# Layer two's weights placed first, the low part issued last, fewer idle products, last stores on three queues

## The chip, the cores and the metric

One core of one Trainium2 chip runs the kernel. Times are device microseconds of one execution; of several runs the median is shown. A profile of one execution was taken beside them.

## The reference

The input `x` has 4 sequences of 4096 tokens with 192 channels, 16384 tokens in all. Three stages follow one another:

```
w = softmax(weight)                                     # 8 heads x 7 taps
x = causal convolution of x with w, each head on its 24 channels
x = (sigmoid(x @ w_gate) * (x @ w_val)) @ w_out         # layer one: 192 -> 1536 -> 192
out = relu(x @ w_in2) ** 2 @ w_out2                     # layer two: 192 -> 2048 -> 192
```

All of it is float32.

## The kernel before

**Precision.** A float32 operand is split into a high part (rounded to the array's fp32r format) and a low part (the rest). A product is taken as high x high, high x low and low x high, which is why each weight tile holds high and low halves and each activation two tensors (`gh` and `gl` for the hidden values).

**Tiling.** 32 tiles of 512 tokens. Layer one goes through 12 *units* of 128 hidden channels for a tile, layer two through 8 units of 256. A unit has a *row* part (`rows`, L477: from the 192 channels to the hidden values, 9 steps) and a *column* part (`cols`, L531: from the hidden values back to 192 channels, 5 steps for each 128 hidden channels, so 5 in layer one and 10 in layer two). Each step is a pair of products, one for partitions 0 to 63 and one for 64 to 127, which run side by side on the array. The two halves sum in different PSUM banks (`acc`, A for output channels 0 to 127, B for the rest), and `fold` (L555) adds them at the end of a phase: ScalarE (ACT) copies one, VectorE (DVE) adds the other, for A and for B, and a third copy and add join B's halves.

**Order.** A phase is all units of one layer for one tile. Layer one runs five phases ahead; then phases of layer one (tile t) and layer two (tile t-5) alternate, and five phases of layer two end the kernel. The main loop (L753) takes unit e: its row products, then `activate`, then the column products that are due, then the *side work* of e. Columns run two units behind: at the first unit of a phase all pending columns of the phase before are run (and its `fold`), at the second none, after that one unit's per unit. PE, ACT and DVE each run their instructions in the order of issue.

`activate` (L518) takes per 128 hidden channels a sigmoid or relu on ACT, a multiplication on DVE (`times`), the high part on ACT (`high`, L508) and the low part on DVE (`low`, L514):

```
for s in acts:
    u.hidden.append(high(s))
    low(u.hidden[-1])
```

Side work is put on units by hand (`side`, `put`, L623 to L628):
- the convolution of the next input tile: a transpose, a first tap on ACT and six taps on DVE, for channels 0 to 127 (A) and, every second tile, for the last 64 channels of two tiles (B): 8 or 16 operations spread over the free units up to `part_at - 1`;
- its high part (ACT), low part (DVE) and `spread` (three DMAs on SyncE's queue, SP, that copy the parts to the other partitions: `x<-x`) at `part_at = at - 4` and the two units behind, where `at` is the first unit of its layer-one phase; loads of the input after it are issued at `part_at`;
- the same parts for layer two's input, on units 4 to 6 of the phase ahead;
- the conversion of layer two's weights (16 jobs of ACT and DVE steps), from unit 2 of the second tile to layer two's first phase. Layer one's weights are converted during the first 12 units, by `convert_and_activate`.

**Memory.** The pool `cp` lays its tiles out in the order of the first request. `w1` (L107) holds layer one's weights, 12 slices of 4608 bytes a partition. Layer two's eight places `u0` to `u7` (`weights2`, `place_of`, L113 to L119; 6144 bytes each) also hold raw weights and scratch while layer one's are converted, so the first request for `u0` to `u4` comes from those loads, behind the small tiles `cw`, `cwr`, `halos`, `xTA`, `xTB`, `gap` and `warm`; the nine small tiles of `conv_weights` (L283) come next, and then `u5` to `u7`.

**Start and end.** PE runs idle products on zeros (`run_idle`, three, then four behind the small products of `conv_weights`) before its first real work, the convolution of the first tiles by products with diagonal matrices (L396). At the end `evac2` (L578) folds, transposes A and B on DVE and stores them by six DMAs on SP.

Of the kernel before, what the change touches and what calls it, by code (L numbers as in the profile page):

```python
# [8 lines left out]
F32 = mybir.dt.float32  # L9
# [4 lines left out]
ALU = mybir.AluOpType  # L14
PSUM = bass.MemoryType.PSUM

P = 128
HB = 64
NT = 512
BLK = 32  # L20
HALVES = (slice(0, HB), slice(HB, P))
# [4 lines left out]
def kernel(  # L26
# [23 lines left out]
    nc = tc.nc  # L50
# [66 lines left out]

    def place_of(i, nm):
        return cp.tile([P, NW2], U32, tag=f"u{i}", name=nm)  # L119

    NRAW = NU2 - 3

# [160 lines left out]
    def conv_weights():  # L283


        mx, z, th, a, b, e, s, r, w = (
            cp.tile([H, k], F32, name=nm)
            for nm, k in (
                ("cmx", 1), ("cz", K), ("cth", K), ("ca", K), ("cb", K), ("ce", K),
                ("cs", 1), ("cr", 1), ("cn", K),  # L290
            )
        )
        nc.vector.tensor_reduce(out=mx, in_=cwr, op=ALU.max, axis=mybir.AxisListType.X)
        nc.vector.tensor_scalar(out=z, in0=cwr, scalar1=mx, scalar2=None, op0=ALU.subtract)
        nc.scalar.activation(th, z, AF.Tanh, scale=0.5)
        nc.vector.tensor_scalar(
            out=b, in0=th, scalar1=-1.0, scalar2=1.0, op0=ALU.mult, op1=ALU.add
        )
        nc.vector.tensor_scalar_add(a, th, 1.0)
        nc.vector.reciprocal(b, b)  # L300
        nc.vector.tensor_tensor(e, a, b, op=ALU.mult)
        nc.vector.tensor_reduce(out=s, in_=e, op=ALU.add, axis=mybir.AxisListType.X)
        nc.vector.tensor_scalar_add(s, s, 1e-9)
        nc.vector.reciprocal(r, s)
        nc.vector.tensor_scalar(out=w, in0=e, scalar1=r, scalar2=None, op0=ALU.mult)
        taken = banks.take("cwp")
        for i in range(2):
            nc.tensor.matmul(
                taken[1][:, i * K : (i + 1) * K], sel[:, i, :], w, start=True, stop=True
            )  # L310
        nc.scalar.copy(cw.rearrange("p i k -> p (i k)"), taken[1][:, 0 : 2 * K])
        banks.give(taken)
# [23 lines left out]
    def load_a(t, eng=None):  # L336
        xin[t] = xp.tile([P, NT], F32, tag="xiA", name="xiA")
        for cb in range(P // BLK):
            load_block(t, xin[t][cb * BLK : (cb + 1) * BLK], cb, eng)
# [168 lines left out]
    def high(s):  # L508
        v = Hidden()
        v.s, v.gh = s, gp.tile([P, NT], F32R, tag="gh", name="gh", bufs=5)  # L510
        nc.scalar.copy(v.gh, s)  # L511
        return v

    def low(v):  # L514
        v.gl = gp.tile([P, NT], F32R, tag="gl", name="gl", bufs=5)
        nc.vector.tensor_tensor(v.gl, v.s, v.gh.bitcast(F32), op=ALU.subtract)  # L516

    def activate(u):  # L518

        u.hidden, acts = [], []  # L520
        for i in range(1 if u.kind == 1 else 2):
            acts.append(act(u, i))
            times(u, acts[-1])
        banks.give(*u.banks)
        for s in acts:
            u.hidden.append(high(s))
            low(u.hidden[-1])

    acc = {}

    def cols(u):  # L531

        key = (u.kind, u.t)
        if u.f == 0:
            acc[key] = [[banks.take(f"acc{nm}") for nm in "AB"] for _ in HALVES]
        sums = acc[key]
        for i, v in enumerate(u.hidden):
            if u.kind == 1:  # L540
                w, lo = w1[:, u.f, NR:], N1 + HB
            else:
                w, lo = weights2(u.f)[1][:, i, :], NO + HB
            wa, wb, wl = w[:, 0:P], w[:, P : 2 * P], w[:, lo : lo + P]
            steps = ((0, wa, v.gh), (0, wa, v.gl), (0, wl, v.gh), (1, wb, v.gh), (1, wb, v.gl))
            first, last = u.f == 0 and i == 0, u.last and i == len(u.hidden) - 1
            for k, (b, wt, m) in enumerate(steps):
                for h, half in enumerate(HALVES):
                    nc.tensor.matmul(  # L549
                        sums[h][b][1], wt[half], m[half],  # L550
                        start=(first and k in (0, 3)), stop=(last and k in (2, 4)),
                    )
        return u.last

    def fold(key, dst_a, dst_b, own):  # L555

        (a0, b0), (a1, b1) = acc.pop(key)
        ca = op.tile([P, NT], F32, tag="c", name="ca")
        cb = op.tile([P, NT], F32, tag="c", name="cb")
        nc.scalar.copy(ca, a1[1])  # L560
        nc.scalar.copy(cb, b1[1])
        nc.vector.tensor_tensor(ca if dst_a is None else dst_a, a0[1], ca, op=ALU.add)
        nc.vector.tensor_tensor(cb, b0[1], cb, op=ALU.add)
        banks.give(a0, b0, a1, b1)
        tb = op.tile([P, NT], F32, tag="oB", name="tb")
        dst_b = cb if dst_b is None else dst_b
        nc.scalar.copy(tb[HALVES[own]], cb[HALVES[1 - own]])
        nc.vector.tensor_tensor(dst_b[HALVES[own]], cb[HALVES[own]], tb[HALVES[own]], op=ALU.add)
        return ca, cb

    def evac1(t):
# [6 lines left out]
    def evac2(t):  # L578

        t0 = tokens(t)  # L580
        ya, yo = fold((2, t), None, None, 0)

        def store(src, cb):
            nc.sync.dma_start(
                out=out[t0 : t0 + NT, cb * BLK : (cb + 1) * BLK].rearrange(
                    "(n t) c -> t n c", t=BLK
                ),
                in_=src.rearrange("t (n c) -> t n c", c=BLK),
            )

        def a():
            o = op.tile([P, NT], F32, tag="oA", name="oA")
            nc.vector.transpose(o, ya)
            for cb in range(P // BLK):
                store(o[cb * BLK : (cb + 1) * BLK], cb)

        def b():
            o = op.tile([P, NT], F32, tag="oB", name="oB")
            nc.vector.transpose(o[0:HB], yo[0:HB])
            for cb in range(HB // BLK):  # L600
                store(o[cb * BLK : (cb + 1) * BLK], P // BLK + cb)

        return [a, b]

# [31 lines left out]
    with tc.manual_schedule():  # L636
# [2 lines left out]
        warm = cp.tile([1, 1], F32, name="warm")  # L639
        nc.gpsimd.memset(warm, 0.0)  # L640
        nc.scalar.activation(warm, warm, AF.Sigmoid)
        load_a(0)
        nc.scalar.dma_start(out=unit, in_=eye)
        load_b(0, nc.gpsimd)
        conv = [convert1(f) for f in range(NU1)]
        for u in range(NU2):
            conv += [convert_rows2(u), convert_cols2(u)]

        idle = gp.tile([P, NT], F32, tag="s", name="idle")
        nc.gpsimd.memset(idle, 0.0)  # L650
        taken = banks.take("idle")

        def run_idle(n):
            for _ in range(n):
                nc.tensor.matmul(taken[1], idle[:, 0:P], idle, start=True, stop=True)  # L655

        for f in range(NRAW):
            conv[f].load()
        load_a(1, nc.gpsimd)
        run_idle(3)  # L660
        conv_weights()
        run_idle(4)
        banks.give(taken)
        a0, b0, (high0, low0, spread0) = prep_x(0, False, True)
        a1, _, parts1 = prep_x(1, True)
# [22 lines left out]
        a1[0]()  # L688
        diagonals(0)

        begin, end = where[1, 1, 2], where[2, 0, NU2 - 2] - 1
        for i, job in enumerate(conv[NU1:]):
            at = begin + i * (end - begin) // (2 * NU2 - 1)
            for s, ops in enumerate(job.stages):
# [6 lines left out]
        for t in range(2, NTILE):  # L701
            at = where[1, t, 0]
            before = starts[starts.index(at) - 1]
            a, b, parting = prep_x(t)
            taps = [o for ab in zip(a, b) for o in ab] if b else a
            part_at = at - 4
            put(taps, free, part_at - 1)
            for i, o in enumerate(parting):
                side[part_at + i].append(o)
            free = part_at + 2  # L710
            if t + 1 < NTILE:
                side[part_at].append(lambda t=t: load_a(t + 1))
                if t % 2:
                    side[part_at].append(lambda t=t: load_b((t + 1) // 2))
# [38 lines left out]
        for e, u in enumerate(units):  # L753
            rows(u)
            if e < NU1:
                convert_and_activate(e, u)
            else:
                activate(u)
            for o in stores:
                o()  # L760
            stores = []
            k = e - max(s for s in starts if s <= e)
            due = len(pending) if k == 0 else 0 if k == 1 else len(pending) - 1
            for _ in range(due):
                v = pending.popleft()
                if cols(v):
                    stores += (evac1 if v.kind == 1 else evac2)(v.t)
            pending.append(u)
            for o in side[e]:
                o()  # L770
        while pending:
            v = pending.popleft()
            if cols(v):
                for o in evac2(v.t):
                    o()
# [39 lines left out]
```

## Time and profile before

| | us |
|---|---|
| median of 3 runs (lowest, highest) | 2420.38 (2417.86, 2421.68) |
| profiled execution, its own time | 2419.86 |
| its span, first to last instruction | 2418.1 |
| PE busy | 2389.6 (99%) |
| PE weight loads (PEld) busy | 1930.4 (80%) |
| DVE busy | 1700.8 (70%) |
| ACT busy | 1301.3 (54%) |

Busy time is the union of an engine's records. A product's record lasts 0.39 us while the next pair starts 0.23 us behind it, so a busy PE says little on its pace; the distance from start to start does. The clock granted to PE (PEclk) is 1.00 at 2.4 GHz and 0.50 at 1.2 GHz.

### The profile page before, as it was taken

What the parts mean: (1) busy time and instruction counts of PE and PEld (TensorE: products, weight loads), DVE (VectorE), ACT (ScalarE), POOL (GpSimd) and SP (SyncE); (2) the same over time, 40 slices, a digit from 0 to 9 for tenths busy, and PEclk for the clock granted to TensorE, in tenths of its full rate; (3) what the DMA queues carried; (4) which work ended last, traced back from release to release, by engine and by line L of the source; (5) the groups of instructions that cost most, each with busy time, mean ns of one, the idle gap of its engine ahead of it and who ended that gap; (6) DMA issues with size and microseconds to landing.
All of it is one profiled execution on the core that took longest, in us unless ns stands there. A gap on an engine that the chain in (4) does not pass through costs nothing.

```text
span 2418.1 us, 49307 instructions
## 1 busy us (share of the span) xinstructions
PE 2389.6 (99%) x20526; PEld 1930.4 (80%) x20526; DVE 1700.8 (70%) x2676; ACT 1301.3 (54%) x2260; POOL 31.6 (1%) x98
## 2 busy tenths in 40 slices
PE   8999999999999999999999999999999999999998
PEld 5677788888888888888888888888888888888886
DVE  7777777777677676676767677776776766666776
ACT  6555555555455555555555555554555555555664
POOL 1000000000000000000000000000000000000000
PEclk9999999999999999999999999999999999999999
DMA  6222221121210111121111211112101111101111
GB/s 154 52 58 50 58 43 24 29 42 25 42 38 21 36 38 30 38 42 22 32 29 38 42 31 26 38 25 43 38 21 36 38 29 38 34 21 27 40 28 27
DMA packets 226896, 92.13 MB, mean 38 GB/s; under 512 B 202856, under 2 KB 214256, under 8 KB 226672
## 3 DMA queue, kind: packets, MB, share of 16 engines
q1 hardware_dynamic: 226272, 88.39, 17.2%
q8 instruction: 160, 2.62, 0.5%
q0 software_dynamic: 256, 0.52, 0.1%
q14 instruction: 64, 0.52, 0.1%
q10 hardware_dynamic: 144, 0.07, 0.0%
HBM read 26.03 MB, written 12.58 MB: 16 GB/s over the span
## 4 chain that ended last, share of the span: by engine, by line
PE 91%; DVE 4%; ACT 2%; issue 1%; DMA 0%; POOL 0%; SPq 0%; DVEq 0%; ACTq 0%; POOLq 0%
PE pg L489 27%; PE accA L549 24%; PE ph L489 22%; PE accB L549 17%; PE pv L489 2%; DVE s L506 1%; ACT gh L511 1%; DVE cvA L387 1%; PE cv L396 1%; DMA x<-x 0%; DVE cvB L387 0%; ACT s L502 0%; DVE gl L516 0%; PE idle L655 0%; ACT cvq L149 0%
## 5 line engine op out<-in xcount | busy, mean ns | idle before, releaser
L549 PE MATMUL accA<-gh,w 64*128 64x512 f32 x3584 | 955.5, 389 | 0.0
L489 PE MATMUL pg<-x,w 64*128 64x512 f32 x3456 | 854.1, 389 | 6.7 <-ACT w L178 3.2
L489 PE MATMUL pv<-x,w 64*128 64x512 f32 x3456 | 851.2, 389 | 7.9 <-DVE s L506 4.4
L511 ACT CAST gh<-s 128x512 fp32r<-128x512 f32 x896 | 555.8, 622 | 544.6 <-DVE s L506 537.9
L516 DVE TENSOR_TENSOR gl<-s,gh 128x512 fp32r<-128x512 f32 x896 | 608.2, 692 | 279.8 <-ACT gh L511 257.7
L489 PEld LDWEIGHTS pg<-x,w 64*128 64x128 f32 x3456 | 635.7, 185 | 130.3 <-ACT w L178 7.0
L549 PEld LDWEIGHTS accA<-gh,w 64*128 64x128 f32 x3584 | 647.5, 184 | 82.3 <-issue 4.5
L489 PEld LDWEIGHTS pv<-x,w 64*128 64x128 f32 x3456 | 635.8, 185 | 35.7 <-DVE s L506 12.7
L489 PE MATMUL ph<-x,w 64*128 64x512 f32 x4608 | 621.2, 391 | 0.0
L489 PEld LDWEIGHTS ph<-x,w 64*128 64x128 f32 x4608 | 471.1, 184 | 102.7
L549 PE MATMUL accA<-gl,w 64*128 64x512 f32 x1792 | 546.3, 389 | 0.4 <-DVE gl L516 0.2
L549 PE MATMUL accB<-gl,w 64*128 64x512 f32 x1792 | 545.9, 389 | 0.0
L549 PE MATMUL accB<-gh,w 64*128 64x512 f32 x1792 | 545.6, 388 | 0.0
L506 DVE TENSOR_TENSOR s<-s 128x512 f32<-128x512 f32 x512 | 330.2, 686 | 157.5 <-ACT s L502 155.9
L502 ACT ACTIVATE s<-ph 128x512 f32<-128x512 f32 x512 | 277.4, 594 | 216.3 <-PE ph L489 215.9
L506 DVE TENSOR_TENSOR s<-pv,s 128x512 f32<-128x512 f32 x384 | 263.2, 686 | 146.0 <-ACT s L502 145.4
L549 PEld LDWEIGHTS accB<-gh,w 64*128 64x128 f32 x1792 | 323.6, 184 | 37.4
L549 PEld LDWEIGHTS accA<-gl,w 64*128 64x128 f32 x1792 | 323.7, 184 | 37.2 <-DVE gl L516 1.1
L549 PEld LDWEIGHTS accB<-gl,w 64*128 64x128 f32 x1792 | 323.1, 184 | 37.5
L502 ACT ACTIVATE s<-pg 128x512 f32<-128x512 f32 x384 | 228.4, 595 | 204.1 <-PE pg L489 192.9
L387 DVE SCALAR_TENSOR_TENSOR cvA<-xTA,cw,cvA 128x512 f32<-128x512 f32 x186 | 138.7, 745 | 3.9 <-ACT cvA L383 3.7
L560 ACT COPY ca<-accA 128x512 f32<-128x512 f32 x64 | 37.3, 583 | 71.6 <-PE accA L549 71.6
(79 smaller groups left out, 758.2 us busy)
## 6 DMA issues: line engine op xcount, KB each, us to landing
x<-x SPq DMA_DIRECT2D x192, 256.0 KB, 3.8
out_dram<-oA SPq DMA_DIRECT2D x128, 64.0 KB, 1.9
xiA<-in_x_dram SPq DMA_DIRECT2D x124, 64.0 KB, 2.8
raw<-in_moe_w_out_dram SPq DMA_DIRECT2D x28, 192.0 KB, 3.5
out_dram<-oB SPq DMA_DIRECT2D x64, 64.0 KB, 1.9
xiB<-in_x_dram SPq DMA_DIRECT2D x60, 64.0 KB, 2.4
raw<-in_moe_w_in_dram SPq DMA_DIRECT2D x16, 192.0 KB, 4.1
raw<-in_moe_w_gate_dram SPq DMA_DIRECT2D x12, 192.0 KB, 3.4
```

Source lines behind the costliest of these rows:

```text
L387: nc.vector.scalar_tensor_tensor(out=st["cv"], in0=st["x"][:, k : k + NT], scalar=cw[:, i, k : k + 1], in1=st["cv"], op0=ALU.mult, op1=ALU ...
L396: nc.tensor.matmul(st["cv"], diagonal(i, k), st["x"][:, k : k + NT], start=(k == 0), stop=(k == K - 1),)
L489: nc.tensor.matmul(u.banks[h][1], w[half, o + c * P : o + (c + 1) * P], xs[1][half, place[n] + p, :], start=(i == 0), stop=(i == len(steps ...
L502: nc.scalar.activation(s, u.banks[i][1], AF.Sigmoid if u.kind == 1 else AF.Relu)
L506: nc.vector.tensor_tensor(s, u.banks[1][1] if u.kind == 1 else s, s, op=ALU.mult)
L511: nc.scalar.copy(v.gh, s)
L516: nc.vector.tensor_tensor(v.gl, v.s, v.gh.bitcast(F32), op=ALU.subtract)
L549: nc.tensor.matmul(sums[h][b][1], wt[half], m[half], start=(first and k in (0, 3)), stop=(last and k in (2, 4)),)
L560: nc.scalar.copy(ca, a1[1])
```

## The change

Five edits. The eight places are requested right behind the definition of `place_of`. `low` is no longer issued in `activate` but at the end of the unit's iteration, behind its due columns, folds and side work (from unit 12 on; the first 12 keep their order). Two idle products go, and the tile of zeros is written on DVE ahead of the first loads. The parts of a tile move from `at - 4` to `at - 5`, and the conversions of layer two begin at unit 8 of the second tile. For the very last unit the column steps are sorted so that B's come first, `fold` then takes B first, and the last six stores go to SP, ACT and POOL.

```diff
+    for u in range(NU2):
+        place_of(u, "free")
...
     def activate(u):
-        u.hidden, acts = [], []
+        acts = []
...
-        for s in acts:
-            u.hidden.append(high(s))
-            low(u.hidden[-1])
+        u.hidden = [high(s) for s in acts]
...
+        order = []
         for i, v in enumerate(u.hidden):
...
+            first = u.f == 0 and i == 0
+            order += [
+                (0, wa, v.gh, first), (0, wa, v.gl, False), (0, wl, v.gh, False),
+                (1, wb, v.gh, first), (1, wb, v.gl, False),
+            ]
+        if u is units[-1]:
+            order.sort(key=lambda step: -step[0])
...
-    def fold(key, dst_a, dst_b, own):
+    def fold(key, dst_a, dst_b, own, b_first=False):
...
+        def sum_a():
+            nc.scalar.copy(ca, a1[1])
+            nc.vector.tensor_tensor(dst_a, a0[1], ca, op=ALU.add)
+
+        def sum_b():
+            nc.scalar.copy(cb, b1[1])
+            nc.vector.tensor_tensor(cb, b0[1], cb, op=ALU.add)
+
+        def join():
+            nc.scalar.copy(tb[HALVES[own]], cb[HALVES[1 - own]])
+            nc.vector.tensor_tensor(
+                dst_b[HALVES[own]], cb[HALVES[own]], tb[HALVES[own]], op=ALU.add
+            )
+
+        for o in (sum_b, join, sum_a) if b_first else (sum_a, sum_b, join):
+            o()
...
-                store(o[cb * BLK : (cb + 1) * BLK], cb)
+                eng = nc.scalar if final and cb % 2 else nc.sync
+                store(o[cb * BLK : (cb + 1) * BLK], cb, eng)
...
-                store(o[cb * BLK : (cb + 1) * BLK], P // BLK + cb)
+                eng = nc.gpsimd if final and cb % 2 else nc.sync
+                store(o[cb * BLK : (cb + 1) * BLK], P // BLK + cb, eng)
...
+        idle = gp.tile([P, NT], F32, tag="s", name="idle")
+        nc.vector.memset(idle, 0.0)
         load_a(0)
...
-        idle = gp.tile([P, NT], F32, tag="s", name="idle")
-        nc.gpsimd.memset(idle, 0.0)
...
+        run_idle(2)
+        conv_weights()
         run_idle(3)
-        conv_weights()
-        run_idle(4)
...
-        begin, end = where[1, 1, 2], where[2, 0, NU2 - 2] - 1
+        begin, end = where[1, 1, 8], where[2, 0, NU2 - 2] - 1
...
-            part_at = at - 4
+            part_at = at - 5
...
             for o in side[e]:
                 o()
+            if e >= NU1:
+                for v in u.hidden:
+                    low(v)
```

## Rows read from the trace of the kernel before

**Rows 1.** The page, busy time: us, share of the span, number of instructions.
```profile
PE 2389.6 (99%) x20526; PEld 1930.4 (80%) x20526; DVE 1700.8 (70%) x2676; ACT 1301.3 (54%) x2260; POOL 31.6 (1%) x98
```
**Rows 2.** Windows: stretch, length, busy us of PE, PEld, DVE, ACT, POOL, clock, DMA.
```profile
74.70:322.48 247.78, 236.92 (x1967) 185.88 (x1964) 185.14 (x326) 132.04 (x237) 4.17 (x16) 0.99 0.22 51
322.48:2228.20 1905.72, 1905.72 (x16643) 1557.91 (x16641) 1329.15 (x2031) 1013.00 (x1754) 20.09 (x64) 1.00 0.16 33
2228.20:2408.56 180.36, 180.36 (x1560) 145.80 (x1558) 126.19 (x195) 105.38 (x184) 0.00 (x0) 1.00 0.14 30
...
118.00:162.00 44.00, 41.47 (x342) 33.07 (x341) 30.28 (x54) 23.06 (x41) 0.50 (x3) 0.96 0.27 58
```
**Rows 3.** Timeline of PE, phase starts: start us, us, engine, line, operation, tiles.
```profile
982.20 0.39 PE L489 MATMUL pg<-x,w 64*128 64x512 f32 x1
...
1022.56 0.63 PE L489 MATMUL ph<-x,w 64*128 64x512 f32 x3
...
1055.50 0.39 PE L489 MATMUL pg<-x,w 64*128 64x512 f32 x1
```
**Rows 4.** Timeline of PE: columns of units 3 and 5 start, rows of 6.
```profile
1044.41 0.62 PE L549 MATMUL accA<-gh,w 64*128 64x512 f32 x2
...
1046.74 0.62 PE L489 MATMUL ph<-x,w 64*128 64x512 f32 x3
...
1048.83 0.39 PE L549 MATMUL accA<-gh,w 64*128 64x512 f32 x1
...
1053.23 0.39 PE L549 MATMUL accA<-gh,w 64*128 64x512 f32 x1
```
**Rows 5.** Timeline of DVE, ACT and PE at the same layer-two phase's start.
```profile
1026.93 1.29 DVE L516 TENSOR_TENSOR gl<-s,gh 128x512 fp32r<-128x512 f32 x2
1028.14 0.69 DVE L562 TENSOR_TENSOR y<-accA,ca 128x512 f32<-128x512 f32 x1
...
1030.11 0.69 DVE L568 TENSOR_TENSOR yb<-cb,tb 64x512 f32<-64x512 f32 x1 [0.69 <-ACT tb L567]
1030.81 0.75 DVE L387 SCALAR_TENSOR_TENSOR cvB<-xTB,cw,cvB 128x512 f32<-128x512 f32 x1
...
1027.40 0.58 ACT L560 COPY ca<-accA 128x512 f32<-128x512 f32 x1
...
1031.36 0.62 PE L549 MATMUL accA<-gl,w 64*128 64x512 f32 x2
```
**Rows 6.** Timeline of DVE and PE at the layer-one phase's start behind it.
```profile
1064.64 0.68 DVE L568 TENSOR_TENSOR cb<-cb,tb 64x512 f32<-64x512 f32 x1 [0.69 <-ACT tb L567]
...
1066.38 0.39 PE L549 MATMUL accA<-gl,w 64*128 64x512 f32 x1
```
**Rows 7.** Waits of PE, 74.7 to 334 us: us in total, times, longest.
```profile
PE pv L489 <- DVE s L506: 4.4, 8, 0.8
PE pv L489 <- DMA x<-x: 3.0, 4, 0.9
PE pg L489 <- DMA x<-x: 2.6, 5, 1.1
```
**Rows 8.** Timeline of PE at the start; DMA engines' busy tenths, 0 to 30 us.
```profile
4.60 5.30 PE L655 MATMUL idle<-idle 128*128 128x512 f32 x6 [4.60 <-POOL idle L650]
...
13.91 6.17 PE L396 MATMUL cv<-xTB,diag 128*128 128x512 f32 x14
...
24.54 0.28 PEld L489 LDWEIGHTS pv<-x,w 64*128 64x128 f32 x1 [0.76 <-DMA x<-x]
...
DMA  0037999899999999999999999998509799888900
```
**Rows 9.** Timeline of DVE and SP's queue at the end; a POOL transfer's landing.
```profile
2411.96 0.69 DVE L593 STREAM_TRANSPOSE oA<-ca 128x512 f32<-128x512 f32 x1
...
2414.72 0.97 SPq L584 DMA_DIRECT2D out_dram<-oB  x2
...
xiB<-in_x_dram POOLq DMA_DIRECT2D x4, 64.0 KB, 2.7
```

More of the change, by code (lines that the diff above doesn't have):

```diff
@@ L544, in cols @@
             wa, wb, wl = w[:, 0:P], w[:, P : 2 * P], w[:, lo : lo + P]
[L545 to L552, printed above, removed]
+            first = u.f == 0 and i == 0
[5 more added lines that the diff above has]
+            order.sort(key=lambda step: -step[0])
+        ends = {step[0]: k for k, step in enumerate(order)} if u.last else {}
+        for k, (b, wt, m, first) in enumerate(order):
+            for h, half in enumerate(HALVES):
+                nc.tensor.matmul(
+                    sums[h][b][1], wt[half], m[half], start=first, stop=ends.get(b) == k,
+                )
         return u.last
-    def fold(key, dst_a, dst_b, own):
+    def fold(key, dst_a, dst_b, own, b_first=False):
         (a0, b0), (a1, b1) = acc.pop(key)
@@ L559, in fold @@
         cb = op.tile([P, NT], F32, tag="c", name="cb")
[L560 to L563, printed above, removed]
+        tb = op.tile([P, NT], F32, tag="oB", name="tb")
+        dst_a = ca if dst_a is None else dst_a
+        dst_b = cb if dst_b is None else dst_b
+        def sum_a():
[8 more added lines that the diff above has]
+                dst_b[HALVES[own]], cb[HALVES[own]], tb[HALVES[own]], op=ALU.add
+            )
+        for o in (sum_b, join, sum_a) if b_first else (sum_a, sum_b, join):
+            o()
         banks.give(a0, b0, a1, b1)
[L565 to L568, printed above, removed]
         return ca, cb
@@ L580, in evac2, with store @@
         t0 = tokens(t)
-        ya, yo = fold((2, t), None, None, 0)
-        def store(src, cb):
-            nc.sync.dma_start(
+        final = t == NTILE - 1
+        ya, yo = fold((2, t), None, None, 0, b_first=final)
+        def store(src, cb, eng):
+            eng.dma_start(
                 out=out[t0 : t0 + NT, cb * BLK : (cb + 1) * BLK].rearrange(
```

## The prediction

> **What bounds the kernel now.** I read the page's engine line first: PE is busy for 2389.6 of 2418.1 us, so what counts is the pitch of its products and the gaps between them [rows 1]. The windows come second. From 322.48 to 2228.20 us PE has no gap at all; from 74.70 to 322.48 it is busy for 236.92 of 247.78 us [rows 2]. Two losses hide beneath the 99%, and both show only when pairs are counted. A "pair" is one weight slice on both row halves.
>
> *Pitch.* The code issues 178 pairs from the first row product of a layer-one phase (982.20) to that of the next layer-two phase (1022.56): 40.36 us, 226.7 ns a pair. From there to 1055.50 it issues 142, in 32.94 us: 232.0 ns [rows 3]. The same array at the same clock is slower in layer two, and the step-by-step rows say where: the ten column pairs of unit 3 take 2.33 us (1044.41 to 1046.74), those of unit 5 take 2.27 (1053.23 to 1055.50) [rows 3, 4]. Only the weight tile differs. By the tile sizes (rounded up to 32 bytes) units 0 to 4 begin 60128 bytes behind the first byte of `w1`, plus multiples of 6144: 224 past a multiple of 512. The nine small tiles of `conv_weights` come in between, so units 5 to 7 begin on a multiple of 512, like every slice of `w1`. The slow ones are the ones off it.
>
> *Gaps.* 982 pairs belong to the stretch 74.70 to 322.48: at 226.7 ns 222.6 us, so 25.2 are lost, 0.75 of them to the pitch of its one layer-two phase. The waits there name DMA x<-x (3.0 and 2.6 us) and DVE s (4.4) [rows 7]. Idle understates it, since a record lasts 0.39 us and the pitch is 0.227; I share the 24.4 us out in proportion: 13.4 to the spread DMAs, 11.0 to the rest.
>
> **The change part by part.** The sum is made against the profiled execution, 2419.86 us (span 2418.1), 0.5 below the median of the three shown.
>
> *Weights ahead.* With the eight places requested right behind `w1` (55296 bytes, 108 x 512) and 6144 = 12 x 512 each, every slice of layer two starts on a multiple of 512 from `w1`. The small tiles have the same sizes and follow in the same order, so the pools behind them start where they did. A layer-two phase behind a layer-one phase then takes 142 x 0.2267 = 32.19 us instead of 32.94: 0.75 x 27 = 20.2. At the end only layer two runs: (1560 - 3) / 2 = 778 pairs (a window counts some three records that only reach into it) in 180.36 us, 176.4 at 226.7: 4.0 [rows 2]. Together **-24.2**. Units 5 to 7's row pairs are slow too, though aligned: unit 6's nine take 2.09 us (1046.74 to 1048.83) [rows 4]. They stand between the columns of units 3 and 4, whose late weight loads run on into them, so I count them as cured. Bounds: 0 if the address isn't the cause, -25 at most.
> The Trainium skill, "TensorE: Matmul & The Clock Gate", Part 2, gives the weight load a read port of its own that takes nothing from the running product, with a time that depends on the number of columns; by it this edit is worth 0 (first rival). The 2.33 against 2.27 us of rows 4 disagrees.
>
> *Low part last.* `activate` issued times, high, low; now low stands on DVE behind the unit's folds and side work. Inside a phase that is free or better: a unit's columns run two units later (over 6 us), and DVE fills its wait for the high part. At a phase start it isn't. In layer two's unit 0, before: gl at 1026.93, then the fold's y add at 1028.14 and yb at 1030.11, then a tap at 1030.81; PE wants the first gl at 1031.36 [rows 5]. After: the fold no longer waits for gl (ca ends at 27.40 + 0.58 = 27.98, so the fold is 0.15 earlier, and 0.05 more from the faster row products); its successor starts 0.70 behind yb, at 1030.61. With a tap in front (0.75, [rows 5]) the first gl ends at 1030.61 + 0.75 + 0.69 = 1032.05; PE, with 27 pairs 5.3 ns shorter, wants it at 1031.21: 0.84 late. Without a tap: 0.09. `put` spreads the 16 operations of an even tile over 18 units and one falls on this one; the 8 of an odd tile miss it. I add 0.1 for the restart (my estimate). Of the 26 such starts after the first, 12 have a tap, 14 none: 12 x 0.95 + 14 x 0.2 = **+14.2**. Behind gl times of unit 1 waits, 1.3 us later than now, but its columns come two units later. At a layer-one start behind layer two the fold's last add (1064.64 + 0.68) leaves 1066.38 - 1065.32 = 1.06 us for one gl of 0.69 and no DVE side work falls there [rows 6]: nothing. Bounds: 0 if folds end earlier than I think, +20 if every start loses what a tapped one does (26 x 0.95, less what the backlog gives back).
>
> *The stretch to 322 us.* `part_at` moves one unit forward, 247.78 / 68 = 3.6 us; the longest wait for the spread was 1.1 [rows 7], so the 13.4 goes. It moves the loads of the next input with it, ahead of the spreads on SP as before. Of the other 11.0 half goes: DVE has work during the high part, but where ACT holds the activation behind a conversion and a part, the order on ACT is as it was. Against it: gl late at six phase starts. With 1.06 us of room and 0.69 for gl, two transposes cost 1.0, one tap 0.4, two taps 1.1, one tap 0.4, three conversion steps (about 1.1 together, an estimate from their share of the tap's width) 0.7, and at the first layer-two start those and a tap 2.0, with restarts 6.2. Net -13.4 - 5.2 + 6.2 = **-12.4**. Bounds -24.4 and +6. Conversions, their raw loads on SP included, start six units later and end at the same unit; same work, so nothing, and if the denser order jams DVE, that is inside the bounds.
>
> *Start.* Idle products, 3 + 4, become 2 + 3, and their zeros are written on DVE, which otherwise waits for the first load, not behind POOL's four issues. Six passes took 5.30 us from 4.60 [rows 8]; four from about 1.4 end at 5, so the convolution on the array can begin up to 5 us before 13.91. But the first unit's row products ended on a DMA x<-x at 24.54, and the DMA engines are 9 tenths busy from 3 us to 20.25 (slices of 0.75 us) with raw weights, which an earlier spread only queues behind. What can go is their gap before the third spread: the slices reading 8, 5 and 0, 0.75 x (0.2 + 0.5 + 1.0) = **-1.3** [rows 8]. Nearest to a DMA bound, so I take that; bounds -5 (all of the array's lead counts) and +1 (the clock's later rise).
>
> *End.* The last unit's B columns come first and end six pairs, 1.36 us, before the last product. Their copy, add, copy, add (0.58 + 0.69 + 0.58 + 0.69, after the ACT and DVE rows of [rows 5]) end 1.2 us behind it, A's add 1.9; A's transpose starts there and not behind all five steps at 2411.96: 1.2 gained. Six issues on SP ran until 2415.69, 3 us past the transpose; on three queues they take half that, but a POOL transfer needs 2.7 us to land, where the kernel ended 2.4 behind SP's last issue [rows 9]. **-2.4**, bounds -3.5 and -1.
>
> Sum: -24.2 + 14.2 - 12.4 - 1.3 - 2.4 = -26.1; 2419.9 - 26.1 = **2394 us**.
>
> **The rivals.**
> *The address does nothing* (the rule above; layer two's own operands set its pitch). For it: no row shows an aligned unit with no slow neighbour in its rows. Against it: unit 5's columns at exactly layer one's pitch. 2394 + 24.2 = 2418. Chance 0.05.
> *gl is nowhere late in the steady part.* For it: 0.09 is small and the fold could gain more from a DVE without gl in front; against it: the 0.84 needs a whole tap to vanish. 2394 - 14.2 = 2380. Chance 0.11.
> *The early stretch keeps its stalls* (ACT's order holds it, new gl waits replace old ones). For it: DVE s is mostly ACT's doing. 2394 + 12.4 = 2406. Chance 0.11.
> *Slower: each late gl takes the clock down.* Place: the starts of layer two. The stretch 118 to 162, with two of the waits for the spread, has a mean clock of 0.96: over 44 us that is 3.5 us at 1.2 instead of 2.4 GHz, 1.76 us lost [rows 2, 7]. At 26 starts 46: 2440. It decides from 15 of them (26.1 / 1.76). Against it: the stalls forecast are below 1 us, and the clock reads 1.00 from 322 us on [rows 2]. Chance 0.03.
>
> **How the numbers follow.** The forecast keeps 0.70, with its own range 2385 to 2404. The range 2378 to 2409 takes in half of the second rival and most of the third: about 0.8. 0.2% (4.8 us) is what a measurement of this kernel can tell from no change: the forecast and the rivals at 2380 and 2406 are faster (0.92), the first is the same (0.05), the last slower (0.03).
>
> **What would show it.** In the profile after: a layer-two pair at 227 ns in the columns of units 0 to 4, and at the phase starts PE waiting on DVE gl, 0.7 to 1 us on every other one, as a new line in the waits; no DMA x<-x there between 75 and 322 us; the granted clock there at 1.00; the first unit's last DMA wait over by 23.2 us and not at 24.54; the last transpose under 2 us behind the last product. I am wrong if layer two's pairs stay at 232 ns, if gl costs nothing or appears at every unit, or if the early stretch still takes 248 us.

## The result, and the profile after

The changed kernel takes 2391.48 us (median of 4 runs, 2390.93 to 2391.85), the kernel before 2420.23 (2417.86 to 2421.68): a ratio of 0.9882, 95% interval 0.9865 to 0.9899. The forecast was 2394, range 2378 to 2409. The profiled execution took 2391.61 us, 28.25 less than the one of before; its span is 2389.5. One of the eight executions of e11 below took 9277.46 us, for a reason that no trace shows; its interval leaves that one out.

Cut at the same points of the program, the two spans compare like this. The cuts are the first row product of the second tile's layer one, the one behind the first phase of layer two, the one of the last five phases, and the last product pair.

| stretch | before, us | after, us | difference | forecast |
|---|---|---|---|---|
| start to the second tile | 74.70 | 74.73 | 0.0 | -1.3 |
| to the end of the first layer-two phase | 247.78 | 228.39 | -19.4 | -12.4 and -0.75 of pitch |
| alternating phases | 1905.72 | 1901.83 | -3.9 | -19.5 of pitch, +14.2 |
| last five layer-two phases | 180.36 | 176.58 | -3.8 | -4.0 |
| last product pair to the end | 9.52 | 7.93 | -1.6 | -2.4 |

The windows of the changed kernel, beside [rows 2] (stretch, length, busy us of PE, PEld, DVE, ACT, POOL, then the clock and DMA):

```profile
74.73:303.12 228.39, 224.48 (x1968) 183.91 (x1965) 183.15 (x327) 134.79 (x238) 8.42 (x16) 1.00 0.23 55
303.12:2204.95 1901.83, 1893.32 (x16642) 1559.20 (x16640) 1312.10 (x2030) 1023.16 (x1754) 30.34 (x63) 1.00 0.16 33
2204.95:2381.53 176.58, 176.58 (x1562) 146.16 (x1558) 124.94 (x196) 107.33 (x185) 0.00 (x0) 1.00 0.14 30
```

The reader sees two things move against each other. The last stretch does the same 779 pairs (counted in the code; the prediction had 778) in 3.8 us less, 226.7 ns a pair, and never waits. The long stretch, without a gap before, now has 8.5 us in which PE is not busy. And the first one reads a clock of 1.00 where [rows 2] read 0.99: the two falls are gone.

The timeline of PE in the phase of [rows 3, 4], columns of unit 3 (from 1023.94) and unit 5 (from 1032.55):

```profile
1023.94 0.39 PE L557 MATMUL accA<-gh,w 64*128 64x512 f32 x2
...
1026.21 0.39 PE L492 MATMUL ph<-x,w 64*128 64x512 f32 x2
...
1032.55 0.39 PE L557 MATMUL accA<-gh,w 64*128 64x512 f32 x2
...
1034.82 0.39 PE L492 MATMUL pg<-x,w 64*128 64x512 f32 x1
```

Both take 2.27 us, where unit 3 took 2.33. The start of that phase, on DVE, ACT and PE, beside [rows 5]:

```profile
1007.01 0.69 DVE L573 TENSOR_TENSOR y<-accA,ca 128x512 f32<-128x512 f32 x1 [1.17 <-ACT ca L572]
...
1008.98 0.69 DVE L581 TENSOR_TENSOR yb<-cb,tb 64x512 f32<-64x512 f32 x1 [0.69 <-ACT tb L580]
1009.68 0.75 DVE L390 SCALAR_TENSOR_TENSOR cvA<-xTA,cw,cvA 128x512 f32<-128x512 f32 x1
1010.35 1.29 DVE L519 TENSOR_TENSOR gl<-s,gh 128x512 fp32r<-128x512 f32 x2
...
1011.15 0.60 ACT L505 ACTIVATE s<-ph 128x512 f32<-128x512 f32 x1 [1.58 <-DVE gl L519]
...
1011.09 0.50 PE L557 MATMUL accA<-gl,w 64*128 64x512 f32 x2 [0.71 <-DVE gl L519]
```

Before, gl led the fold by 1.2 us; now it stands behind fold and tap. The columns began at 1010.00, so the second pair, due 0.227 later, came 0.87 late, and the pair behind it lost another 0.11. That is 0.98 us at each of the 12 starts with a tap; the 13 odd ones lose 0.21 and the last 0.31, 14.8 us in all. Most of the column pairs behind these two still take 0.231 to 0.236 us on average, another 1.2 us: with them the stretch is 15.9 us longer than its 8320 pairs at 226.7 ns. The waits of PE, first from 72 to 320 us, then from 330 to 2381 (us in total, times, longest), beside [rows 7]:

```profile
PE accA L557 <- DVE gl L519: 3.7, 4, 1.7
PE pg L492 <- DVE w L192: 0.2, 1, 0.2
...
PE accA L557 <- DVE gl L519: 8.5, 12, 0.7
```

Neither DMA x<-x nor DVE s is left, and the 12 tapped starts are there by number. (Of the 14 others, 13 are 0.1 us late, less than the 0.17 by which a record outlasts the pitch, and don't show.)

### The profile page after: what moved, and what is told of

Its sections match the earlier page's. It is cut to its first block, busy times and chain, and to the rows that moved or that the text cites. A ratio compares the mean times of both kernels' runs of the same rounds, so it can differ in the third digit from the quotient of the medians.

```text
span 2389.5 us, 49288 instructions
## 1 busy us (share of the span) xinstructions
PE 2362.3 (99%) x20522; PEld 1930.7 (81%) x20522; DVE 1680.4 (70%) x2677; ACT 1315.6 (55%) x2260; POOL 46.4 (2%) x98
## 4 chain that ended last, share of the span: by engine, by line
PE 78%; issue 16%; DVE 3%; ACT 2%; DMA 1%; SPq 0%; POOLq 0%; DVEq 0%; ACTq 0%; POOL 0%
PE pg L492 28%; PE accA L557 20%; PE ph L492 14%; PE accB L557 13%; PE pv L492 1%; ACT gh L514 1%; DVE s L509 1%; ACT s L505 1%; DVE cvA L390 0%; DVE y L573 0%; DVE gl L519 0%; ACT tb L580 0%; DVE cb L577 0%; ACT ca L572 0%; DVE yb L581 0%
## 5 line engine op out<-in xcount | busy, mean ns | idle before, releaser
L557 PE MATMUL accA<-gh,w 64*128 64x512 f32 x3584 | 699.7, 387 | 0.0
L492 PE MATMUL ph<-x,w 64*128 64x512 f32 x4608 | 558.9, 386 | 0.0
L492 PEld LDWEIGHTS ph<-x,w 64*128 64x128 f32 x4608 | 432.3, 184 | 90.2
L557 PEld LDWEIGHTS accA<-gh,w 64*128 64x128 f32 x3584 | 337.1, 184 | 73.2 <-issue 4.5
L557 PE MATMUL accA<-gl,w 64*128 64x512 f32 x1792 | 353.2, 390 | 12.4 <-DVE gl L519 12.2
L557 PE MATMUL accB<-gh,w 64*128 64x512 f32 x1792 | 349.9, 387 | 0.0
L557 PE MATMUL accB<-gl,w 64*128 64x512 f32 x1792 | 349.7, 387 | 0.0
L557 PEld LDWEIGHTS accA<-gl,w 64*128 64x128 f32 x1792 | 168.5, 184 | 58.7 <-DVE gl L519 25.1
L557 PEld LDWEIGHTS accB<-gl,w 64*128 64x128 f32 x1792 | 168.5, 184 | 35.3
L557 PEld LDWEIGHTS accB<-gh,w 64*128 64x128 f32 x1792 | 168.4, 184 | 35.3
```

The source lines that it names most:

```text
L492: nc.tensor.matmul(u.banks[h][1], w[half, o + c * P : o + (c + 1) * P], xs[1][half, place[n] + p, :], start=(i == 0), stop=(i == len(steps ...
L557: nc.tensor.matmul(sums[h][b][1], wt[half], m[half], start=first, stop=ends.get(b) == k,)
```

## The experiments

Each is an edit of the changed kernel except the first, which is one of the kernel before. Ratios and their 95% intervals are against the kernel before, run beside each; its median moved by up to 1.2 us from one group of experiments to another. "After", "less" and "more" refer to the changed kernel's 2391.48 us, from which a difference of about 1 us tells nothing by itself.

**e1: the weights alone.** The kernel before, with `for u in range(NU2): place_of(u, "free")` behind `place_of`, and nothing else.

> The kernel before with one edit alone: the eight places requested right behind w1. Theory (the address sets the pitch): every layer-two pair at 226.7 ns, unit 5 to 7's row pairs too, 24 to 25 us less, about 2396 us; the stalls up to 300 us stay as before, 25 us in all. Rival (layer two's own operands set the pitch, and the rest of the change brought the 29 us): pairs stay at 232 ns and the time at 2420. Second rival (the faster pitch uncovers waits for DVE at the phase starts): 226.7 ns but 2400 or more.

Measured: 2395.48 us against 2420.48, ratio 0.9897 (0.9883 to 0.9912): 25.0 us, and 23.9 between the spans of the two profiled executions. The windows of this kernel, at the same cuts:

```profile
74.57:321.82 247.25, 236.51 (x1967) 195.89 (x1965) 184.62 (x325) 132.04 (x237) 4.02 (x15) 0.99 0.22 50
321.82:2208.11 1886.29, 1886.19 (x16642) 1558.66 (x16639) 1327.92 (x2032) 1012.75 (x1754) 20.26 (x64) 1.00 0.16 34
2208.11:2384.68 176.57, 176.57 (x1560) 145.93 (x1558) 126.18 (x195) 104.97 (x184) 0.00 (x0) 1.00 0.14 30
```

19.4 and 3.8 us go from the last two, 0.5 from the first, which keeps its stalls. No wait takes the place. Unit 6's rows, and the columns behind them, in the phase of [rows 4]:

```profile
1038.96 0.39 PE L492 MATMUL ph<-x,w 64*128 64x512 f32 x1
...
1041.01 0.39 PE L552 MATMUL accA<-gh,w 64*128 64x512 f32 x1
```

Its nine row pairs take 2.05 us instead of 2.09, on a place that was aligned before and after. The rival that the address does nothing is out.

**e9, e10, e11: the weights 32, 64 and 128 bytes further on.**

```diff
+    cp.tile([P, 8], F32, name="shift")       # 16, 32 for 64 and 128 bytes
     for u in range(NU2):
         place_of(u, "free")
...
-    cp.tile([P, 64], F32, name="gap")
+    cp.tile([P, 56], F32, name="gap")        # 48, 32
```

> The changed kernel with all eight layer-two places 32 bytes further on (the gap tile that much smaller, so that the pools behind stay). Theory (a weight slice off its place is slow, whatever the unit): every layer-two pair, units 5 to 7 included, at 232 to 235 ns, 4864 pairs x 6 = 29 us more, less some of the gl waits, which a slower array gives time: 2415 to 2421 us. Rival (224 bytes was special): 226.7 ns and 2391 us.

> The same with 64 bytes. If what counts is a multiple of 64 bytes: 226.7 ns a pair and 2391 us. If it is 128 bytes or more: layer two slow in all units, 2415 to 2421 us, or in between.

> The same with 128 bytes. If a multiple of 64 or 128 bytes counts: 226.7 ns and 2391 us. If it is 256 or 512: slow, 2415 to 2421 us.

Measured: 2420.21, 2420.59 and 2417.14 us; against the kernel before 1.0005 (0.9995 to 1.0015), 1.0005 (0.9995 to 1.0015) and 0.9988 (0.9977 to 0.9999). All three lose the gain. With 32 bytes, the columns of unit 5, on PE's timeline:

```profile
1040.86 0.40 PE L558 MATMUL accA<-gh,w 64*128 64x512 f32 x2
...
1043.19 0.38 PE L493 MATMUL pg<-x,w 64*128 64x512 f32 x1
```

2.33 us for the ten pairs that took 2.27 before and after: the unit that was fast in the kernel before is slow once it is moved, in the same program position and on the same data. Layer one, whose slices stayed, kept 227 ns. So the place decides. 64 bytes past a multiple of 512 are no better than 32 (233.3 ns a pair in the last five phases with both), 128 hardly (232.4). Whether 256 would do, and whether the place itself counts or its distance from the other operand's, was not run. One rival can be put aside from the traces: in the kernel before and in e1 one row half runs a step behind the other through the alternating phases, after and in e9 to e11 both start together; yet e1 and the changed kernel are fast, the kernel before and e9 slow. What the 6 ns are spent on no run shows: the records of the weight loads last 184 ns in the slow kernels as in the fast ones.

**e2: the low part back in `activate`.**

```diff
                 activate(u)
+                for v in u.hidden:
+                    low(v)
...
-            if e >= NU1:
-                for v in u.hidden:
-                    low(v)
```

> The changed kernel with the low part back in activate. Theory (low last costs 14.8 us at the layer-two starts and 5.6 at the first six starts, and gains only the waits for DVE s before 300 us, 9 to 10 us, and 1.3 us of late gl there): no PE wait on gl from 320 us on, waits for DVE s back before it, no DMA x<-x, about 2391.5 - 20.4 + 11 = 2382 us. Rival (low last is also what brings the parts of a tile early enough, and the earlier unit alone does not): the DMA x<-x waits come back too, 13 us more, 2395 us.

Measured: 2389.15 us (0.9869, 0.9854 to 0.9884), between the two. The alternating phases take 1885.87 us, 16.0 less than after: no wait for gl is left there, as the theory had it. But the early stretch takes 242.03 and not 228.39. The largest waits of PE in it, and of DVE:

```profile
PE pv L492 <- DVE s L509: 5.4, 11, 1.4
PE accA L557 <- DVE gl L519: 1.1, 5, 0.2
PE accA L557 <- ACT gh L514: 0.8, 2, 0.6
...
DVE gl L519 <- ACT gh L514: 42.5, 62, 0.7
DVE s L509 <- ACT s L505: 12.6, 17, 2.0
```

No DMA x<-x, so the rival falls too. What the theory had too small is the price of the old order in a full stretch: 62 times DVE stands for up to 0.7 us between `times` and `low` with conversions and taps queued behind it, and the backlog makes gh and gl late at the *ends* of phases: 5.8 us by the products' starts, where the theory had 1.3. Low last is worth 13.6 us net there.

**e3: low in `activate` at the first unit of a phase only.**

```diff
                 activate(u)
+                if e in starts:
+                    for v in u.hidden:
+                        low(v)
...
-            if e >= NU1:
+            if e >= NU1 and k:
                 for v in u.hidden:
                     low(v)
```

> The changed kernel with low in activate at the first unit of each phase only, last everywhere else. Theory: all gl waits at phase starts go, 14.8 + 5.6 us, and the waits for DVE s before 300 us stay away, so about 2371 us. Rival (with low ahead of it the fold ends later, and the wait moves to the PSUM banks or to the next unit's products): the gl waits go and others of the same size come, 2388 to 2392 us.

Measured: 2370.28 us (0.9793, 0.9777 to 0.9809), 21.2 less than after. DVE and PE at the same phase start:

```profile
995.39 1.29 DVE L519 TENSOR_TENSOR gl<-s,gh 128x512 fp32r<-128x512 f32 x2
996.60 0.68 DVE L573 TENSOR_TENSOR y<-accA,ca 128x512 f32<-128x512 f32 x1
...
998.56 0.69 DVE L581 TENSOR_TENSOR yb<-cb,tb 64x512 f32<-64x512 f32 x1 [0.69 <-ACT tb L580]
...
999.69 0.47 PE L557 MATMUL accA<-gl,w 64*128 64x512 f32 x2
```

gl is ahead of the fold again, which ends 0.22 us ahead of the columns (999.25 against 999.47; after, 0.33); PE doesn't wait. The early stretch takes 223.91 us. Of DVE's waits in it, the first is what is left of the 42.5 us in e2:

```profile
DVE gl L519 <- ACT gh L514: 10.3, 15, 0.7
DVE s L509 <- ACT s L505: 31.6, 42, 2.0
```

The two effects of low last are thus apart. Inside a phase it is worth 18.1 us in the early stretch (242.03 in e2, 223.91 here) and nothing in the alternating phases (1885.87 in both). How is argued: it fills DVE's hole in front of gl, though 19 of the 32 us come back as DVE's wait for the sigmoid. At a phase's start it puts work with a long wait in front of an operand that is due. The place where it costs can be left out.

**e4: the parts back at `at - 4`.**

> The changed kernel with part_at = at - 4 as before. Theory A (the unit gained is what removed the DMA x<-x waits): they come back before 300 us, with the fall of the clock behind two of them, 10 to 13 us more, 2402 to 2405 us. Theory B (the order with low last already brings a tile's own low part earlier on DVE, by the 0.7 us of one gl and the 0.7 us of idle before it): waits of at most 0.3 us are left, 2391 to 2394 us.

Measured: 2404.33 us (0.9933, 0.9918 to 0.9948), as theory A had it, and yet not for its reason. The early stretch is only 5.2 us longer (233.62); x<-x is waited for at the start of two phases and not of four, with one fall of the clock:

```profile
PE pv L492 <- DMA x<-x: 2.4, 3, 1.5
...
PE pg L492 <- DMA x<-x: 0.2, 1, 0.2
```

The other 8.5 us lie in the alternating phases (1910.30), where no spread is late. With `part_at` one unit later `put` lays the taps of odd tiles on the first layer-two unit as well. DVE and PE at such a start, the phase after the one shown above:

```profile
1090.69 0.68 DVE L581 TENSOR_TENSOR yb<-cb,tb 64x512 f32<-64x512 f32 x1 [0.68 <-ACT tb L580]
1091.30 0.74 DVE L390 SCALAR_TENSOR_TENSOR cvA<-xTA,cw,cvA 128x512 f32<-128x512 f32 x1
1091.96 1.28 DVE L519 TENSOR_TENSOR gl<-s,gh 128x512 fp32r<-128x512 f32 x2
...
1092.69 0.50 PE L557 MATMUL accA<-gl,w 64*128 64x512 f32 x2 [0.59 <-DVE gl L519]
```

0.75 us late, and 0.87 lost with the pair behind instead of 0.21, 13 times. So each theory holds for a part: the spreads of two phases are in time without the unit gained, the others need it, and it kept 13 taps off these starts. What brought the first two in time, low last or the later conversions of layer two, which this kernel keeps too, no run sets apart.

**e5: the start of before.** Three and four idle products, zeros on POOL.

> The changed kernel with the start of before: zeros on POOL, three and four idle products. Theory (the spread waits in the queue behind raw loads whatever the array does, and what is won is lost in unit 1 to a longer half clock): half clock for 7 us from about 23 us and not 10, unit 2's rows at 32.0 us in both, 2391 to 2392 us. Rival (the prediction's term): unit 2 comes 1.3 us later, 2392.8 us.

Measured: 2390.89 us (2390.61 to 2391.78), the same as after. Unit 2's rows start at 32.77 us instead of 32.00, its half clock lasts from 24.9 to 31.7 us and not from 20.8 to 31.1; the median shows nothing of the 0.77 us. The start's edits are worth nothing that can be told.

**e6: fewer raw loads ahead of the spread.**

```diff
-        for f in range(NRAW):
+        for f in range(3):
             conv[f].load()
...
         spread0()
-        conv[NRAW].load()
+        for f in range(3, NRAW + 1):
+            conv[f].load()
```

> The changed kernel with three raw weight slices loaded ahead and the fourth and fifth only behind the first tile's spread. Theory (queue): the spread lands 3 to 3.5 us after its issue at 14.7 us, not 6.8; unit 0's rows end at 22 to 23 us, not 25.2; units 1 to 11 follow as much earlier, 2388 to 2389 us. Rival (conversions of layer one's weights bound units 1 to 11 from the first activation on, or slices 3 and 4 now come late): unit 0 is earlier, unit 12 is not, 2391 us or more.

Measured: 2387.45 us (2387.40 to 2387.70; 0.9868, 0.9853 to 0.9883), 4.0 less. After, unit 0's fourth and fifth steps on PE's timeline:

```profile
21.57 0.79 PE L492 MATMUL pg<-x,w 64*128 64x512 f32 x1 [1.41 <-DMA x<-x]
...
22.80 0.79 PE L492 MATMUL pv<-x,w 64*128 64x512 f32 x1 [0.44 <-DMA x<-x]
```

and with three loads ahead the fourth step and the unit's first activation:

```profile
19.45 0.39 PE L492 MATMUL pg<-x,w 64*128 64x512 f32 x1
...
22.30 0.60 ACT L505 ACTIVATE s<-pg 128x512 f32<-128x512 f32 x1 [0.74 <-PE pg L492]
```

The first spread was issued at the same time (14.85 against 14.72 us), the fourth step no longer waits for it, the activation comes at 22.30 instead of 25.34, and unit 12 at 71.22 instead of 74.73. The spread had stood in the queue behind raw weights, and everything behind unit 0 follows it.

**e7: the end of before.** No sort, `b_first=False`, all stores on `nc.sync`.

> The changed kernel with the end of before: column steps in the old order, A folded first, all six stores on SP. Theory: from the last product's end to the span's end 8.9 us and not 7.55, 1.4 us more, 2392.8 us. Rival (the B-first order costs the array something before the last product, so that the net is nothing): 2391.5 us.

Measured: 2392.09 us (2391.54 to 2392.18). In its trace 8.92 us lie between the last product's end and the span's (8.91 before) and 7.55 after: 1.4. The medians show 0.6 of it, since the starts of the runs scatter by as much; the trace decides for the theory.

**e8: idle products to hold the clock.** One more behind the first convolution on the array and two ahead of unit 0's fourth step.

> The changed kernel with three idle products more, one behind the first convolution on the array and two ahead of unit 0's fourth step, where it waits for the spread. Theory (the half clock is what ate the start's gain): the clock stays at 2.4 GHz from 10 us on, unit 0's last five steps and unit 1's nine take 0.23 us each and not 0.43, unit 2's rows start 2 to 3 us earlier, 2388.5 to 2389.5 us. Rival (from unit 1 on ACT's and DVE's conversions bound the units): the clock stays up and unit 2 still starts at 32 us, 2391 us; or it falls all the same, 2391 us.

Measured: 2388.44 us, but 2387.74 to 2392.00, and the profiled execution is the one at 2392.00. In it the clock rose at 4.4 us and fell at 24.9 all the same, and unit 2 began at 33.02. What the clock did in the faster ones no trace shows. Inconclusive; that the half clock took the start's gain is argued, not shown.

**e12: e3 and e6 together.**

> The changed kernel with low in activate at the first unit of each phase only, and with three raw weight slices ahead of the first spread. Theory: the two gains lie in different stretches and add, 21.2 us in the phases and 4.0 in the start: 2391.5 - 25.2 = 2366 us. Rival (with the start 4 us earlier layer two's conversions or the first phases give part back): 2368 to 2370 us.

Measured: 2367.18 us (2366.08 to 2367.47; 0.9784, 0.9768 to 0.98): 24.3 less than after, 53 less than before. The early stretch takes 223.90 us, the alternating phases 1885.86, as in e3, and unit 12 begins at 69.97. They add but for 0.9 us, too little to tell the theory from its rival; this version beats both kernels.

## Why the prediction was right, step by step

*Pitch, -24.2.* Right in size and cause: -25.0 alone (e1), and the places 32 to 128 bytes off bring the old time back (e9 to e11). (-4.0 for the last five phases would be -3.8 with 779 pairs, as measured.) Units 5 to 7's row pairs were cured with their neighbours, 231 to 226.7 ns (e1). The reason given, late weight loads that run on into them, no run shows: unit 7's nine row pairs read 225 to 236 ns to the last, and the columns of unit 5 right behind them 227. The Trainium skill, "TensorE: Matmul & The Clock Gate", Part 2, gives the weight load a read port of its own that takes nothing from the running product, and by that this edit would be worth nothing. These runs disagree: with slices of the same columns a pair takes 6 ns more when they lie 32, 64, 128 or 224 bytes past a multiple of 512.

*Low part last, +14.2.* Right: 14.8 us of late gl, 0.98 with a tap and 0.21 without against 0.95 and 0.2, and none at layer-one starts in the alternating phases. Taken away as a whole (e2, e3) it brings 16.0; the 1.2 us of slower pairs behind were not in the sum.

*The stretch to 322 us, -12.4.* The term that was mis-sized: -18.7 without the pitch. Late gl cost 5.5 us at six starts, forecast 6.2. The waits for the spread went, as forecast, but the unit earlier was not alone in it: with it none come back even with low early (e2), without it (e4) only 5 us do. The step that was off is the half of the DVE s waits that the prediction left in place, 5.2 us, because ACT's order is unchanged; they went to nothing. (Its 5.2 is half of 10.5, DVE s alone; half of the 11.0 that it names is 5.5.) That the place of low inside a phase decides it is shown, 18.1 us between e2 and e3. That DVE's idle time in front of gl is the way, 42.5 us with low early and 10.3 with the split, fits and is not shown by itself. The prediction read "DVE s" as ACT's doing from its wait for the sigmoid, and did not ask where DVE's own backlog came from.

*Start, -1.3.* Wrong by its whole size: 0. The bound was named rightly, a spread behind raw loads, and e6 takes it away for 4.0 us. The first unit's last wait for the spread was over at 22.80 us, sooner than the 23.2 that were to show it. But the 0.46 us by which unit 1 started earlier (26.55 against 27.01) were gone at unit 2 (32.00 in both): unit 1's stretch reads a clock of 0.59, in the kernel before 0.69. That the clock is what took them is argued, not shown (e8). After, then before:

```profile
26.55:32.00 5.45, 5.43 (x20) 3.29 (x20) 3.98 (x9) 3.38 (x6) 0.00 (x0) 0.59 0.27 86
```

```profile
27.01:32.00 4.99, 4.80 (x21) 2.95 (x22) 3.99 (x9) 3.38 (x6) 0.00 (x0) 0.69 0.49 137
```

*End, -2.4.* Too large: -1.6 from the last pair, of which 0.2 is one row half's last product, which began 0.23 us behind the other's before and doesn't after; -1.4 from the last product's end, as in e7. The end of the changed kernel, and the landings of its last six stores, then of the same stores before (issues, KB, median us):

```profile
2383.20 0.68 DVE L573 TENSOR_TENSOR ca<-accA,ca 128x512 f32<-128x512 f32 x1
2383.91 0.71 DVE L613 STREAM_TRANSPOSE oA<-ca 128x512 f32<-128x512 f32 x1
...
out_dram<-oA SPq DMA_DIRECT2D x2, 64.0 KB, 2.1
out_dram<-oA ACTq DMA_DIRECT2D x2, 64.0 KB, 2.5
out_dram<-oB POOLq DMA_DIRECT2D x1, 64.0 KB, 2.8
out_dram<-oB SPq DMA_DIRECT2D x1, 64.0 KB, 2.7
```

```profile
out_dram<-oA SPq DMA_DIRECT2D x4, 64.0 KB, 1.9
out_dram<-oB SPq DMA_DIRECT2D x2, 64.0 KB, 1.9
```

A's transpose starts 2.0 us behind the last product (2381.91) and not 2.8, 0.8 gained of the 1.2 expected. (2.8 less the 1.9 that the prediction worked out would have been 0.9.) From there to the end it takes 5.55 us instead of 6.12: the last issue ends 1.5 us sooner behind the transpose, but the stores, issued closer together, land 2.1 to 2.8 us behind their issue and not 1.9, SP's own too.

The errors had different signs: 6.3 us too little gained in the early stretch, 2.1 too much at start and end and 1.4 in the alternating phases. That the sum came within 2.5 us of the result owes something to luck.

## What to carry to other kernels

Count products and divide: a busy engine can hide a pitch that depends on where an operand lies, and rows of the same kernel with differently placed tiles show it before anything is built. When work is moved behind other work on an in-order engine, ask for each position in the loop when its result is due; here the move paid inside a phase, cost at a phase's first unit, and the split version kept the gain without the cost. A wait named after an engine can be that engine's own backlog: look at what it stood idle for one instruction earlier.

## What the runs showed of the hardware

- The pitch of a pair with 64 x 128 fp32r weights and 512 columns is 226.7 ns with the slice on a multiple of 512 bytes from `w1`, and 232 to 233 ns on average 32, 64, 128 or 224 bytes past it; nearly all single pairs lie between 225 and 241. The slowness reaches into aligned neighbours (231 ns in the rows of units 5 to 7 before). 256 bytes was not run.
- A pair that waits for its operand costs the pair behind it 0.11 us more (0.335 to 0.342 instead of 0.227), and most of the column pairs behind that one ran at 0.231 to 0.236 us.
- With the same first instructions the clock first rose at 4.4 to 11.1 us in the profiled runs (4.4 in e8, 9.5 in e3, 10.6 after, 11.1 in e4), and unit 0's rows began between 15.9 and 18.7 us; unit 12 began at 73.9 to 75.7 in all of them (after, e2 to e4 and e7 to e11).
